# A recurrent attention layer and a mixture of experts in one kernel: the order of chunks 2 to 21, as written or from a list made at build time

## The chip, the cores and the metric

The kernel runs on one NeuronCore of a Trainium2 chip. The metric is the device time of one execution in microseconds (us); lower is better. A core has five engines, each of which takes its own instructions strictly in the order of the program: PE (matrix products, which write to the PSUM banks), DVE (vector work), ACT (scalar engine: copies and activations), POOL (vector work without access to PSUM, and DMA issues) and SP (DMA issues only). Engines wait for each other through semaphores that the Tile framework places from the data that instructions read and write.

## What is computed

The first half is a recurrence over 768 steps, for 4 batches and 8 heads, with a 40x40 state each; the second half sends every row of its result through a top-1 mixture of 8 experts:

```python
for t in range(768):
    y[:, :, t] = einsum('bhd,bhde->bhe', r_t, state)
    Sa = einsum('bhde,bhe->bhd', state, a_t)
    state = state * w_t[:, :, None, :] - einsum('bhd,bhe->bhde', Sa, b_t)
    state = state + einsum('bhd,bhe->bhde', v_t, k_t)
x = y as 3072 rows of 320
rows with x @ w_skip > 0: e = argmax(x @ w_gate), g = softmax weight of e
    out = x + g * (relu(x @ w1[e]) @ w2[e]);   other rows: out = x
```

## The kernel before, in words

The 768 steps are cut into 24 chunks of 32 steps. Inside a chunk the recurrence becomes matrix products, and only the state is handed from chunk to chunk. All heads are worked on at once, in two halves, x = 0 and x = 1 (of the head pairs), which are independent of each other.

For each chunk c and half x there is a chain. `rs` (L288) multiplies the state with the reads; its result goes from PSUM into the operand tile R1 (L292 on DVE when c is even, L293 on ACT when it is odd). `ux` (L302) multiplies R1, ACT copies the result (L304), `uq` (L313) applies the inverted triangular matrix, ACT writes it back into R1 in four copies (L315) and POOL masks it (L317). `sst` (L325, L330) makes the next state, which is copied out by L334 (DVE) or L335 (ACT), and by L338 (ACT); the next chunk's `rs` needs these. `yy` (L348) gives the output, which DVE scales (L352) and SP stores (L353).

Beside the chain runs preparation for later chunks, in pieces of two chunks (index h): DVE scans the decays (L114, L126), POOL multiplies keys and a (L143, L151), `m1` makes the triangular matrices on PE (L163), ACT and DVE empty its bank (L165, L174), POOL masks (L170) and SP moves the result by four DMAs of 32 KB (L172). `kbt` (L185, emptied by four ACT copies, L188), `wtt` (L197, emptied by L199) and `m2` (L207, emptied by four copies, L209) transpose and multiply other operands. For each piece of four chunks, `tinv` inverts the triangular matrices on DVE by 30 steps of forward substitution in two column blocks, X0 in PSUM (`px`) and Xi in SBUF (`M`): a product (L228) and a subtraction (L230) for each block and step. `route` scores finished rows for the experts (transposition L628, scores L636, selection L644 to L681 on DVE) and scatters them (L684).

The order of all this is written out by hand in the loop over c (L465): pieces of preparation stand between the links of the chain, the steps of `tinv` are given out by `T()`, those of `route` by `RP()`. PE, ACT and DVE issue in exactly the written order (a manual schedule); for POOL and SP the framework's own scheduler sets the order.

Eight PSUM banks are handed out by `Ring`, round robin, by purpose: two banks `pc` for rs, ux and uq; two `ps` for sst; one `py` for yy; one `px` for tinv; and two banks `pq` for everything else (m1, kbt, wtt, m2, route). A task that takes a bank waits until the one that had it before has been copied out.

Chunks 0 and 1 follow a start-up section of their own; chunks 22 and 23 run while the first expert's weights are split. Then come the experts (L744), whose matrix products fill PE.

## Time and profile before

| | us |
|---|---|
| median of three runs | 665.6 (663.45 to 666.89) |
| the profiled execution | 663.83 |
| its span, first to last instruction | 662.1 |
| busy in the span: PE / DVE / ACT / POOL | 515.5 / 489.7 / 419.5 / 324.2 |

The output rows of chunk c are scaled on DVE (L352) in the pass of the loop after it. The first of these 24 instructions starts at 92.5 us, the 21st at 481.8 and the last at 520.6, so one can cut the span by them: up to 92.9 us start-up and chunk 0; then twenty passes up to 482.3; then the end of the attention; and from about 530 the experts. In the listings a line such as `L228` is the line of the kernel printed above; `M<-M,px` reads "written tile from read tiles". PE's products of 16 small matrices appear as 32 records.

### The profile page before, as it was taken

What the parts mean: (1) busy time and instruction counts of PE and PEld (TensorE: products, weight loads), DVE (VectorE), ACT (ScalarE), POOL (GpSimd) and SP (SyncE); (2) the same over time, 40 slices, a digit from 0 to 9 for tenths busy, and PEclk for the clock granted to TensorE, in tenths of its full rate; (3) what the DMA queues carried; (4) which work ended last, traced back from release to release, by engine and by line L of the source; (5) the groups of instructions that cost most, each with busy time, mean ns of one, the idle gap of its engine ahead of it and who ended that gap; (6) DMA issues with size and microseconds to landing.
All of it is one profiled execution on the core that took longest, in us unless ns stands there. A gap on an engine that the chain in (4) does not pass through costs nothing.

```text
span 662.1 us, 33508 instructions
## 1 busy us (share of the span) xinstructions
PE 515.5 (78%) x14772; PEld 432.2 (65%) x14772; DVE 489.7 (74%) x1182; ACT 419.5 (63%) x1151; POOL 324.2 (49%) x246
## 2 busy tenths in 40 slices
PE   4777776676776787767785877878886899999995
PEld 1543456565664576656664666666775599999995
DVE  7998697858997479973999736864166457888881
ACT  5463674586965778567785677887885354555540
POOL 5481951648545375553946442223132155666661
PEclk8786895799977898878889689988788999999998
DMA  7473665352443525335253333453365266676210
GB/s 227 152 242 107 166 207 160 104 177 63 139 125 107 174 63 150 109 112 168 83 156 88 107 113 81 140 153 113 105 178 167 73 183 201 214 229 216 77 48 24
DMA packets 67446, 91.06 MB, mean 138 GB/s; under 512 B 32564, under 2 KB 54657, under 8 KB 65806
## 3 DMA queue, kind: packets, MB, share of 16 engines
q1 hardware_dynamic: 62350, 74.05, 38.1%
q0 software_dynamic: 4944, 14.80, 6.6%
q8 instruction: 118, 1.93, 1.2%
q14 instruction: 34, 0.28, 0.1%
HBM read 74.03 MB, written 17.08 MB: 138 GB/s over the span
## 4 chain that ended last, share of the span: by engine, by line
PE 24%; DVE 11%; ACT 8%; issue 5%; DMA 2%; POOL 1%; SPq 0%; POOLq 0%; DVEq 0%; ACTq 0%
PE pc L782 5%; PE ps L793 4%; PE px L782 3%; ACT R1t L315 2%; PE py L793 2%; ACT L2t L188 2%; DVE M L228 2%; PE ps L325 2%; DVE ti L789 2%; PE pc L313 1%; PE pc L288 1%; DVE M L230 1%; PE ps L330 1%; ACT SS L338 1%; ACT R1t L209 1%
## 5 line engine op out<-in xcount | busy, mean ns | idle before, releaser
L317 POOL TENSOR_TENSOR R1t<-R1t,mc 64x512 f32<-64x512 f32 x46 | 60.5, 1315 | 104.7 <-ACT R1t L315 72.6
L315 ACT COPY R1t<-pc 32x288 f32<-32x288 f32 x192 | 74.9, 390 | 20.7 <-PE pc L313 17.6
L730 POOL TENSOR_TENSOR WL<-WR,WH 128x1280 fp32r<-128x1280 f32 (+1 forms) x21 | 57.7, 2782 | 8.7 <-ACT WH L729 8.6
L188 ACT COPY L2t<-pq 64x160 f32<-64x160 f32 x184 | 52.8, 287 | 7.5 <-PE pq L185 5.1
L684 POOL DMA_INDIRECT xg<-XS,ix x24 | 25.5, 1064 | 64.3 <-DMA xg<-XS,ix 26.0
L325 PE MATMUL ps<-R1t,L2t 128*40 128x40 f32 x1472 | 48.2, 221 | 11.0 <-issue 5.3
L143 POOL TENSOR_TENSOR WR<-WR,M 128x1024 f32<-128x1024 f32 (+1 forms) x19 | 44.2, 2332 | 25.8 <-DVE M L114 19.7
L228 DVE TENSOR_TENSOR M<-M 128x22 f32<-128x22 f32 (+10 forms) x110 | 55.0, 500 | 0.0
L325 PEld LDWEIGHTS ps<-R1t,L2t 128*40 128x40 f32 x1472 | 39.3, 132 | 18.9 <-ACT R1t L315 8.9
L338 ACT COPY SS<-ps 40x320 f32<-40x320 f32 x92 | 38.7, 420 | 19.9 <-PE ps L330 18.5
L209 ACT COPY R1t<-pq 32x128 f32<-32x128 f32 x184 | 47.2, 256 | 5.5 <-PE pq L207 1.3
L288 PE MATMUL pc<-rvt,SS 128*40 128x32 f32 x1472 | 44.9, 216 | 7.2 <-issue 4.8
L288 PEld LDWEIGHTS pc<-rvt,SS 128*40 128x40 f32 x1472 | 38.3, 135 | 15.4 <-issue 7.8
L330 PE MATMUL ps<-L2t,R1t 128*40 128x40 f32 x1472 | 42.9, 218 | 6.5 <-issue 6.4
L313 PE MATMUL pc<-UXs,TB 32*32 32x72 f32 x1536 | 43.1, 255 | 6.0 <-issue 5.9
L330 PEld LDWEIGHTS ps<-L2t,R1t 128*40 128x40 f32 x1472 | 38.2, 134 | 7.3 <-issue 7.2
L230 DVE TENSOR_TENSOR M<-M 128x22 f32<-128x22 f32 (+10 forms) x110 | 40.8, 371 | 0.0
L230 DVE TENSOR_TENSOR px<-px,M 128x168 f32<-128x168 f32 (+8 forms) x150 | 39.1, 260 | 1.4
L729 ACT CAST WH<-WR 128x1024 fp32r<-128x1024 f32 (+1 forms) x35 | 39.6, 1132 | 0.0
L313 PEld LDWEIGHTS pc<-UXs,TB 32*32 32x32 f32 x1536 | 32.1, 122 | 11.4 <-issue 8.9
L789 DVE CAST ti<-xe 128x2 int32<-128x2 f32 x8 | 39.3, 4911 | 0.2
L174 DVE STREAM_TRANSPOSE M<-pq 128x128 f32<-128x128 f32 x40 | 12.1, 308 | 36.9 <-ACT M L165 24.3
(240 smaller groups left out, 1529.3 us busy)
## 6 DMA issues: line engine op xcount, KB each, us to landing
rvt<-rv POOLq DMA_DIRECT2D x21, 512.0 KB, 3.9
WR<-kb SPq DMA_DIRECT2D x10, 1024.0 KB
WR<-w SPq DMA_DIRECT2D x16, 640.0 KB
WR<-w SPq DMA_DIRECT2D x16, 512.0 KB
M<-wt SPq DMA_DIRECT2D x9, 520.5 KB
M<-at SPq DMA_DIRECT2D x8, 512.0 KB
WR<-w SPq DMA_DIRECT2D x16, 256.0 KB
R1t<-vt SPq DMA_DIRECT2D x48, 80.0 KB
```

Of the source, the lines that this page charges most:

```text
L188: A.copy(L2[x][h%NL2][64-64*x:128-64*x,c,bb*4:bb*4+4,:],pt[64*c:64*c+64,:,64*x:64*x+40])
L209: A.copy(R1[x][c%NR1][ao[x]:ao[x]+32,4*b:4*b+4,40:72],Pp[32*b:32*b+32])
L228: V.tensor_tensor(tv,NLt[:,j,j+1:32].unsqueeze(2).broadcast_to([128,n,k]),X[:,j,lo:hi].unsqueeze(1).broadcast_to([128,n,k]),ALU.mult)
L230: for tv,xv in q: V.tensor_tensor(xv,xv,tv,ALU.subtract)
L288: TE.matmul(RS[s,v,:],SS[x][:,b//2,v,:],rr[:,b%2,2*hh+x,:],start=True,stop=True)
L313: TE.matmul(UQ[q,hh,:],Tb[q,x*8+hh*2+c%2,:],UXd[x][q,hh,:],start=True,stop=True)
L315: A.copy(R[uu,4*b:4*b+4,:],UQ[32*b:32*b+32,:,:])
L317: (V if c==NC-1 else G).tensor_tensor(R[pq,:,40:72],R[pq,:,40:72],mQ[pq].unsqueeze(1).broadcast_to([64,16,32]),ALU.mult)
L325: TE.matmul(ST[s,v,:],l2[:,cc,u,:],R[:,u,0:40],start=True,stop=True)
L330: TE.matmul(S2[s,v,:],R[:,u,0:40],l2[:,cc,u,:],start=True,stop=True)
L730: def low(s,E,o,x,h): E.tensor_tensor(s.R(o),x,h,ALU.subtract)
L782: for n,(a,b) in enumerate(mm): TE.matmul(ph[:,g],R(a),R(b),start=n==0,stop=n==7)
```

## The change

Nothing that is computed changes. A recording layer is put between the loop and the engines (`Rec`). From c == 2 on, a call such as `V.tensor_tensor(...)` is no longer issued but written down as a task, with the parts of tiles that it reads and writes and a price from a table of formulas (`cost`); matmuls that follow each other into the same bank are one task. When c reaches 22, `flush` works out which task depends on which (`deps`), gives each a key (its place in the writing, times the busiest engine's work per task, less the priced length of the longest path from it to the end of the recording), and runs a list schedule (`plan`): each engine in turn takes the ready task with the lowest key, or one that fits in front of it with at most 1.0 us of delay. Then all tasks are issued in the order of their planned starts. POOL's order is now also fixed by this; SP's still comes from the framework's scheduler, which now sees the DMAs in the order of the plan.

Banks are handed out by the plan too. The rings for `pc`, `ps` and `pq` become three tiles of two banks each; a recorded task that wants a bank may get any of these six, with one pair held back for the oldest task that has none yet. `px` and `py` stay as they are. The pools of small tiles become fixed tiles used in turn (`Static`).

```diff
+class Rec:
+    HOP=0.12; PW=1.25
...
+    def cost(s,e,op,w,r,a):
...
+        if 'dma' in op:
+            by=4*n*min(128,w[0].ap[0][1])
+            return (0.06 if e=='S' else 1.0 if 'ind' in op else 0.6),2.0+by/2.6e5
+        if e=='P': return (0.145 if op=='transpose' else max(0.0005*sz(w[0]),0.058)),0
+        if e=='A': return 0.15+0.00085*n,0
+        if e=='G': return (0.08+n*0.0008 if op=='memset' else 0.65+0.0015*n),0
...
+        if op=='tensor_tensor': return 0.14+0.00105*n*(1 if ps else 1.6),0
...
+    def call(s,e,op,fn,a,k):
+        if not s.on: return fn(*a,**k)
...
+        if e=='P' and L and L.e=='P' and L.out==W[0][0]:
+            L.calls.append((fn,a,k,own)); L.W+=W; L.R+=R; L.d+=d; return
+        t=Task(); t.e,t.op,t.calls,t.W,t.R,t.d,t.lat,t.out=e,op,[(fn,a,k,own)],W,R,d,lat,W[0][0] if W else None
+        s.tasks.append(t)
...
+        while done<N:
+            best=None
+            for e in 'VAGPS':
+                c=[]
+                for i in pool[e] if not keep else [i for i in pool[e] if i==seq[e][nxt[e]]]:
+                    w=want(i) if T[i].al else (0.0,None)
+                    if w is None: continue
+                    c.append((max(free[e],rdy[i],w[0]),i,w[1]))
+                if not c: continue
+                c.sort(key=lambda x:s.key[x[1]])
+                x=c[0]
+                while True:
+                    f=[y for y in c if y[0]<x[0] and y[0]+T[y[1]].d<=x[0]+s.LET]
+                    if not f: break
+                    x=f[0]
+                if best is None or x[0]<best[0]: best=x+(e,)
...
+    LET=1.0; FAR=1.0
+    def keys(s):
+
+        w=max(sum(t.d for t in s.tasks if t.e==e) for e in 'VAGP')/len(s.tasks)
+        s.key=[i*w-s.FAR*t.up for i,t in enumerate(s.tasks)]
+    def flush(s):
+        s.on=False
+        s.deps(); s.keys(); s.plan()
...
+        for i in sorted(range(len(s.tasks)),key=lambda i:(s.st[i],i)):
+            for fn,a,k,own in s.tasks[i].calls: fn(*[at(x,own) for x in a],**{n:at(x,own) for n,x in k.items()})
...
-    ps_c,ps_s,ps_y,ps_p,ps_x=(Ring(pp,n,k) for n,k in (("pc",2),("ps",2),("py",1),("pq",2),("px",1))); m.ps=ps_p
+    PQ,PC,P2=(pp.tile([128,2,512],F32,name=n) for n in ("pq","pc","ps")); PY,PX=(pp.tile([128,512],F32,name=n) for n in ("py","px"))
+    rec.pairs={t.name:t for t in (PQ,PC,P2)}
+    two=lambda t: [t[:,q] for q in range(2)]
+    ps_c,ps_s,ps_p=(Ring(two(t),rec) for t in (PC,P2,PQ)); ps_y,ps_x=Ring([PY]),Ring([PX]); m.ps=ps_p
...
             ph,j=divmod(c,4)
+            if c==2: rec.on=True
             if c==20: m.load(0)
             if c==22:
+                with tc.manual_schedule(engines={ET.Pool}): rec.flush()
                 mp.__exit__(None,None,None)
```

Three places show what it does to the order. A row is one instruction, or several equal ones (`x16`); in the changed kernel every recorded instruction carries line 225, that of the issuing loop, or 115.

First PE, in a chunk in the middle, with four transpositions of `kbt` (shape 128x104). Before, each link of the chain has its fixed banks, and the rest shares `pq_104` and `pq_105`:

```order
L313 MATMUL pc_99<-UXs,TB 32x72 x16
L185 MATMUL pq_105<-mc,WR 128x104 x4
L348 MATMUL py_103<-L2t,R1t 32x40 x16
L636 MATMUL pq_104<-wg,xT 32x9 x12
L302 MATMUL pc_100<-R1t,WR 32x72 x16
L185 MATMUL pq_105<-mc,WR 128x104 x4
L325 MATMUL ps_102<-R1t,L2t 40x40 x16
L330 MATMUL ps_101<-L2t,R1t 40x40 x16
L207 MATMUL pq_104<-rvt 32x32 x16
```

and with the change, at the like place (`pq`, `pc` and `ps` name pairs of banks here):

```order
L225 MATMUL pq<-UX_447,TB 32x72 x16
L225 MATMUL ps<-WR,L1t 32x64 x16
L225 MATMUL pc<-mc,WR 128x104 x4
L225 MATMUL py<-L2t,R1t 32x40 x16
L225 MATMUL pq<-rvt_146 32x32 x16
L225 MATMUL pq<-mc,WR 128x104 x4
L225 MATMUL pc<-L2t,R1t 40x40 x16
L225 MATMUL pc<-R1t,L1t 32x72 x16
```

The transpositions and `m1` (32x64) now go into `pc`, `ps` and `pq` alike, and the two products of sst (40x40) no longer stand together.

Second DVE, in the midst of `tinv`. Before, the four instructions of a step alternate between the two blocks, so that an instruction never follows the one whose result it needs:

```order
L228 TENSOR_TENSOR M<-M,px_106 128x168
L228 TENSOR_TENSOR M<-M 128x130
L230 TENSOR_TENSOR px_106<-px_106,M 128x168
L230 TENSOR_TENSOR M<-M 128x13x10
L228 TENSOR_TENSOR M<-M,px_106 128x160
L228 TENSOR_TENSOR M<-M 128x132
L230 TENSOR_TENSOR px_106<-px_106,M 128x160
```

With the change:

```order
L225 TENSOR_TENSOR M<-M,px 128x168
L225 TENSOR_TENSOR px<-px,M 128x168
L225 TENSOR_TENSOR R1t<-ps,D_498 40x8x40 x2
L225 TENSOR_TENSOR M<-M 128x126
L225 TENSOR_TENSOR XS_1341<-py,WT_475 128x320
L225 TENSOR_TENSOR M<-M 128x14x9
L225 TENSOR_TENSOR M<-M,px 128x160
```

The product for `px` and its subtraction now stand next to each other, and the block in `M` runs several steps behind. Over the recorded chunks `tinv` has 508 such instructions in both orders; 70 of them follow directly the one whose result they need before, 154 now.

Third SP, in a stretch with one piece's slices (L172, from `at` into the tile that m1 reads next) and the loads of v (L107). Before:

```order
L172 DMA L1t<-M 32x256 x4
L107 DMA R1t<-vt 32x16x40
L94 DMA M<-wt 128x1041
L353 DMA out<-XS 4x32x320
L353 DMA X<-XS 4x32x320
L172 DMA L1t<-M 32x256 x4
L107 DMA R1t<-vt 32x16x40
```

With the change:

```order
L225 DMA R1t<-vt 32x16x40
L225 DMA WR<-M 32x256 x2
L225 DMA out<-XS_1342 4x32x320
L225 DMA X<-XS_1342 4x32x320
L225 DMA WR<-M 32x256 x4
L225 DMA M<-zer 32x1024
L225 DMA WR<-M 32x256 x2
L225 DMA R1t<-vt 32x16x40
```

The slices of the two halves x are mixed with stores and with each other; a load of v still stands behind slices.

## The prediction

> **What bounds the kernel now.** I read the page first, then busy time by stage, then four passes of the loop one by one, then what PE waited for.

> ```profile
> span 662.1 us, 33508 instructions
> PE 515.5 (78%) x14772; PEld 432.2 (65%) x14772; DVE 489.7 (74%) x1182; ACT 419.5 (63%) x1151; POOL 324.2 (49%) x246
> ```

> The busy times by stage (columns: stretch, its length, busy PE, weight loads, DVE, ACT, POOL, then granted PE clock, DMA share, GB/s):

> ```profile
> 0.00:92.90 92.90, 63.22 (x1686) 39.18 (x1688) 79.39 (x114) 51.32 (x138) 56.84 (x49) 0.83 0.59 181
> 92.90:482.30 389.40, 291.64 (x10956) 242.65 (x10951) 286.05 (x876) 281.44 (x853) 181.39 (x151) 0.87 0.42 122
> 482.30:530.00 47.70, 37.43 (x1207) 29.07 (x1207) 28.08 (x87) 26.42 (x81) 12.54 (x10) 0.89 0.49 144
> 530.00:662.10 132.10, 123.19 (x936) 121.31 (x936) 96.16 (x108) 60.33 (x81) 73.42 (x37) 0.98 0.48 149
> ```

> The change touches the second row alone. There no engine is full: PE 75%, DVE 73%, ACT 72%. The experts below are bound by PE (93%) and stay. So the question is what 389.4 us hold beside work. Four passes, one piece of `tinv`, show it, and with them the last pass of the stage:

> ```profile
> 218.10:244.10 26.00, 19.57 (x725) 16.40 (x725) 13.59 (x28) 17.73 (x53) 13.17 (x12) 0.87 0.43 123
> 244.10:259.30 15.20, 11.75 (x433) 9.75 (x425) 14.93 (x50) 13.18 (x41) 9.13 (x8) 0.89 0.48 139
> 259.30:286.50 27.20, 18.44 (x739) 15.35 (x733) 26.68 (x70) 17.35 (x53) 16.22 (x14) 0.86 0.43 126
> 286.50:300.20 13.70, 10.95 (x361) 8.92 (x361) 8.95 (x41) 9.80 (x32) 4.75 (x4) 0.78 0.33 91
> 466.00:482.30 16.30, 14.23 (x483) 12.09 (x478) 2.05 (x12) 14.56 (x44) 2.80 (x4) 0.79 0.36 107
> ```

> In the second and third pass DVE is full (41.6 of 42.4 us); in the first and fourth it is busy for 22.5 of 39.7 and nothing is full. The load is uneven, not too large: over the four passes PE has 60.7, DVE 64.2, ACT 58.1 us of work in 82.1. The last row shows that a pass can run with PE and ACT at 87% and 89%.

> What PE waited for in the stage (in total, times, longest):

> ```profile
> PE pq L628 <- DVE M L174: 12.3, 5, 4.1
> PE pq L163 <- issue: 11.1, 10, 3.3
> PE pc L302 <- DVE R1t L292: 11.0, 7, 2.9
> PE pq L207 <- ACT L2t L188: 9.7, 8, 1.4
> PE ps L325 <- issue: 5.3, 5, 2.1
> PE pq L185 <- ACT L2t L188: 5.2, 8, 1.6
> PE pq L636 <- ACT WT L199: 5.2, 5, 1.7
> PE py L348 <- issue: 5.0, 4, 2.0
> PE pc L288 <- issue: 4.8, 4, 1.6
> PE ps L325 <- ACT R1t L315: 4.0, 11, 0.5
> PE pc L302 <- issue: 3.9, 3, 1.8
> PE pc L313 <- issue: 3.6, 5, 1.4
> PE pq L671 <- ACT WT L199: 2.6, 9, 0.3
> PE pq L163 <- DVE M L174: 1.6, 1, 1.6
> ```

> Three kinds. Six rows say "issue": 33.7 us, PE waiting for nothing that the profile shows. Six name a bank `pq` that another task's copy has not emptied: 12.3 + 9.7 + 5.2 + 5.2 + 2.6 + 1.6 = 36.6. Two are links of the chain, 11.0 + 4.0 = 15.0. Smaller rows are left out; these 85 us stand against 97.8 idle (389.4 less 291.6).

> **The change part by part.** No instruction is added or removed, so PE's 291.6 us and the "issue" time stay: it touches only the 36.6 and 15.0 us, and may disturb what is hidden now.

> *Banks.* A task that found `pq` full now finds any of six banks, in a planned order. The rows that wait for ACT sum to 22.7; ACT has 108 us idle in the stage, so its copies can be in time, and I take 18 off (bounds 0 and 22.7). The rows that wait for DVE's L174 (13.9) are of another sort: that instruction stands behind `tinv` work while DVE is full, and a fuller PE does not change this. With six banks the PE task need not follow it, but the m1 behind it must; I take 6 off (bounds 0 and 13.9). Sum 24.

> *Chain.* The plan lets an evacuation with a long path behind it pass `tinv` steps. That can take at most the 15.0 us of L292 and L315. An evacuation still waits for the DVE instruction that is running, and the four L315 copies are work, not waiting. I take a third, 5 (bounds 0 and 15).

> *DVE neighbours.* The price table does not know that a DVE instruction directly behind the one whose result it needs starts later:

> ```profile
> 126.54 0.23 DVE L228 TENSOR_TENSOR M<-M,px 128x88 f32<-128x88 f32 x1
> 126.70 0.21 DVE L228 TENSOR_TENSOR M<-M 128x60 f32<-128x60 f32 x1
> 126.83 0.24 DVE L230 TENSOR_TENSOR px<-px,M 128x88 f32<-128x88 f32 x1
> 126.99 0.20 DVE L230 TENSOR_TENSOR M<-M 128x60 f32<-128x60 f32 x1
> 127.12 0.23 DVE L228 TENSOR_TENSOR M<-M,px 128x80 f32<-128x80 f32 x1
> ...
> 129.23 0.20 DVE L228 TENSOR_TENSOR M<-M,px 128x48 f32<-128x48 f32 x1
> 129.47 0.22 DVE L230 TENSOR_TENSOR px<-px,M 128x48 f32<-128x48 f32 x1
> 129.72 0.20 DVE L228 TENSOR_TENSOR M<-M,px 128x40 f32<-128x40 f32 x1
> ```

> Alternating, starts are 0.145 us apart (0.58 for four); in a single chain 0.245, though the tiles are smaller. So a neighbour costs 0.1 or a little more, say 0.11. The new order has 84 more of them (154 less 70): 9 us of DVE time. They are on the path only while DVE is full, which is half of the four passes (42.4 of 82.1): 4 us added (bounds 0 and 9). [...]

> *Clock.* After the longest of the L628 waits PE runs slowly for a while:

> ```profile
> 125.71 0.90 PE L628 MATMUL pq<-mc,XS 128*128 128x128 f32 x3 [4.14 <-DVE M L174]
> 126.54 1.28 PE L288 MATMUL pc<-rvt,SS 128*40 128x32 f32 x32
> ...
> 237.68 0.81 PE L288 MATMUL pc<-rvt,SS 128*40 128x32 f32 x32
> ...
> 125.70:129.00 3.30, 3.29 (x68) 2.65 (x69) 3.20 (x20) 1.26 (x4) 0.78 (x1) 0.50 0.49 147
> ```

> The granted clock was 0.50 there, and the same group took 1.28 us in place of 0.81. A stretch of 3.3 us so loses about 1.3 us; if all five of these waits went, 6 us; I take 3 (bounds 0 and 6). [...]

> *Loads.* SP's order changes too. PE's list has no row above 0.3 us that ends on a DMA, so I add nothing; what it would cost is a rival below.

> Sum against the profiled execution: 663.8 - 18 - 6 - 5 + 4 - 3 = 635.8. The median of the runs lies 1.8 us above that execution (665.6 against 663.83), so the forecast is 637.6, about 638. The stage would then last 361 us, in which PE's work and all its "issue" waits fill about nine tenths, against 84% now.

> **The rivals.**

> *The clock stays up.* If PE's idle pieces get so short that the half clock mostly disappears, more is won. A mean of 0.87 is a quarter of the stage, some 100 us, at half clock. If 60 us of these went, at three quarters busy and with 1.28 against 0.81 for the same work, 60 x 0.75 x 0.37 = 17 us would go beside the 28, less the 3 counted already: 624. For it: only the long waits have a slow stretch right behind them. Against: the last pass above has PE at 87% and a clock of 0.79.

> *DVE holds the pace.* `tinv` must be done before the next piece, and the DVE rows that lie between two scalings of output (L352) are almost as many as before in each pass. If the two full passes keep their length, only the other half gains: 24 + 5 by 39.7/82.1 is 14, less the whole 9 us of neighbours: 659 + 2 = 661, or with two thirds of that gain 665, that is, no change.

> *SP holds the chain.* The plan prices an issue on SP at 0.06 us. The trace:

> ```profile
> SPq L172 <- POOL M L170: 95.4, 15, 13.2
> ...
> 235.10 2.50 SPq L172 DMA_DIRECT2D L1t<-M  x4
> 237.69 0.59 SPq L107 DMA_DIRECT2D R1t<-vt  x1
> ```

> An issue takes about 0.6, and SP already stands for 6.4 us on average (95.4/15) before a group of slices, with the load of v for the next chunk behind it. Without v neither `ux` nor `sst` of that chunk can start, and all engines stop behind them. Today the load comes early enough. If the fuller order starts a chunk sooner but POOL's mask (L170) is no sooner, part of these waits lands on the chain. From 28/15 = 1.9 us each the change is slower; if half of each arrives, 15 x 3.2 = 48, it is 638 + 48 = 686. For it: stores now stand among the slices, ahead of the loads. Against: the loads have a whole pass of lead, and POOL is under half busy.

> **How the numbers follow.** Forecast (638, own range 622 to 653): 0.58. Clock stays up (624 and below): 0.15. No change (DVE): 0.11. Slower (SP, or another queue in the same way): 0.16. A measurement of this kernel tells a difference from about 0.5%, 3.3 us. Faster is then 0.73, same 0.11, slower 0.16. With every gain at its bound (22.7 + 13.9 + 15 + 6) the time is 606 + 2; I set the low end at 606. The high end is 668, which holds the no-change case and leaves most of the slower one out: about 0.05 and 0.14 outside.

> **What would show it.** Right: the passes of the recorded chunks last 17 to 19 us on average in place of 19.5; in PE's waits the rows that now end on L188, L199 and L174 shrink from 36.6 to about 12, and "issue" stays near 40; the experts keep their 132 us. For the clock: a granted clock above 0.92 in the stage. For DVE: two passes of four still as long as now, with DVE full. For SP: PE rows `pc` waiting for a DMA of v. I would be wrong altogether if waiting on "issue" grew with a denser PE, since nothing in the trace says what it is, or if new head-of-line waits between ACT and PE took the place of the bank waits.

## The result, and the profile after

The changed kernel takes 810.67 us (median; 806.66 to 816.17), the kernel before, run beside it, 664.72 us (663.45 to 666.89). The ratio is 1.22, with a 95% interval of 1.2105 to 1.229. The forecast was 638 us, faster. The profiled execution took 813.72 us. All times and ratios from here on are those of runs within 1.5% of the fastest of their kernel, since a few executions fall into a slower state.

The head of the page, and of its table of the span in 40 slices the rows for TensorE's work and granted clock:

```profile
span 812.0 us, 33448 instructions
PE 579.8 (71%) x14772; PEld 485.2 (60%) x14772; DVE 455.5 (56%) x1182; ACT 423.3 (52%) x1151; POOL 317.2 (39%) x246
...
PE   4687668676767667677768777776676777668776
...
PEclk8876767589767869876876869595687899889889
```

Busy times by stage, cut at the same instructions as before (start-up to the first scaling of output, the recorded chunks, the end of the attention, the experts):

```profile
0.00:105.70 105.70, 69.89 (x1672) 43.28 (x1673) 76.89 (x115) 52.89 (x138) 56.88 (x49) 0.75 0.53 162
105.70:550.80 445.10, 321.15 (x11005) 268.17 (x11002) 292.87 (x882) 283.24 (x851) 176.60 (x151) 0.77 0.36 108
550.80:609.50 58.70, 41.67 (x1172) 32.30 (x1168) 25.52 (x78) 25.99 (x81) 10.52 (x9) 0.73 0.36 107
609.50:812.00 202.50, 147.09 (x940) 141.41 (x940) 60.21 (x109) 61.17 (x83) 73.21 (x37) 0.88 0.32 98
```

Against the stages before, the start-up is 12.8 us longer, the recorded chunks 55.7, the end of the attention 11.0 and the experts 70.4. Most of the loss (94.2 of 149.9 us) therefore lies where nothing is recorded and every engine has the written order. In the experts, the last slices of the PE row show 6 to 8 tenths where there was a 9 throughout.

What TensorE waited for in the whole span (us in total, times, longest), largest rows:

```profile
PE pq L225 <- ACT R1t L225: 33.9, 36, 6.6
PE pc L115 <- DVE hL L115: 26.3, 12, 3.5
PE pq L115 <- DVE xH L115: 19.3, 7, 2.8
```

and all of its waits in the experts before:

```profile
PE pq L759 <- DMA xe<-xg: 1.0, 3, 0.6
PE px L782 <- DVE xL L730: 0.2, 1, 0.2
```

L225 issues what was recorded, L115 what was not. The second and third row are the experts': 45.6 us of waits for DVE instructions `hL` and `xH` that had no row before. The place where one of them falls, DVE's row first, then TensorE's:

```profile
617.13 0.68 DVE L115 SCALAR_TENSOR_TENSOR hL<-pc,hH 128x512 fp32r<-128x512 f32 x1
...
614.00 0.28 PE L115 MATMUL pc<-xH,WH 128*128 128x256 f32 x1
614.11 0.28 PE L115 MATMUL pc<-xH,WL 128*128 128x256 f32 x1
617.87 0.58 PE L115 MATMUL pc<-xH,WH 128*128 128x256 f32 x1 [3.48 <-DVE hL L115]
618.25 0.42 PE L115 MATMUL pc<-xH,WL 128*128 128x256 f32 x1
618.47 0.41 PE L115 MATMUL pc<-xH,WH 128*128 128x256 f32 x1
618.68 0.41 PE L115 MATMUL pc<-xH,WL 128*128 128x256 f32 x1
```

TensorE fills the first bank `pc` until 614.4. The products that follow go into the *second* bank `pc`, which is empty, and need nothing of `hL`; still they begin when DVE has finished reading the first bank, at 617.81. Before, the same two groups ran back to back, without a wait (the last product of the first and the first of the second):

```profile
533.71 0.28 PE L782 MATMUL pc<-xH,WL 128*128 128x256 f32 x1
533.82 0.28 PE L782 MATMUL pc<-xH,WH 128*128 128x256 f32 x1
```

In the change the rows behind the wait are 0.21 us apart instead of 0.12. The granted clock (the third number from the end) ahead of the wait's end and behind it, and of the same work before:

```profile
613.60:616.90 3.30, 0.79 (x7) 0.58 (x6) 2.74 (x3) 2.03 (x3) 0.00 (x0) 1.00 0.47 115
617.90:621.40 3.50, 3.50 (x16) 3.50 (x17) 0.00 (x0) 0.00 (x0) 0.00 (x0) 0.50 0.56 174
```

```profile
531.90:535.70 3.80, 3.80 (x34) 3.75 (x33) 1.94 (x3) 3.08 (x4) 0.00 (x0) 1.00 0.67 191
```

So the loss has two parts: the waits, and the half clock behind them. In the experts the work of PE grew by 23.9 us (147.09 against 123.19) for the same products, at a mean granted clock of 0.88 against 0.98, in the recorded chunks by 29.5 (321.15 against 291.64), at 0.77 against 0.87: a third of the whole loss. The wait lasted 3.48 us, but by the trace's clock records the clock fell at 617.0, 0.9 us before the wait ended, and TensorE had been busy for 0.79 of the 3.30 us ahead: that stretch was not wholly idle. The last section has more on this.

The instructions as built show why: each carries the semaphores it waits for. Before, none of TensorE's waits on ACT, DVE or POOL is owed to an instruction that only touches another bank. In the change 149 of some 520 are. It holds the other way too: 69 of ACT's 389 waits for TensorE and 18 of DVE's 115 end with products into the other bank; before, none did. The change cuts the six banks `pq`, `pc`, `ps` out of three tiles of two banks, and the framework that places the semaphores keeps the order of writes and reads by tile, so that a write into one half of a tile waits for the readers of the other half.

### The profile page after: what moved, and what is told of

The parts are those of the page before. It is cut to its first block, busy times and chain, and to the rows that moved or that the text cites. A ratio compares the mean times of both kernels' runs of the same rounds, so it can differ in the third digit from the quotient of the medians.

```text
span 812.0 us, 33448 instructions
## 1 busy us (share of the span) xinstructions
PE 579.8 (71%) x14772; PEld 485.2 (60%) x14772; DVE 455.5 (56%) x1182; ACT 423.3 (52%) x1151; POOL 317.2 (39%) x246
## 3 DMA queue, kind: packets, MB, share of 16 engines
q8 instruction: 118, 1.93, 1.0%
## 4 chain that ended last, share of the span: by engine, by line
PE 28%; ACT 12%; DVE 6%; issue 3%; DMA 1%; SPq 0%; POOL 0%; POOLq 0%; DVEq 0%; ACTq 0%
PE pc L115 7%; PE ps L115 6%; PE pq L225 6%; ACT R1t L225 4%; PE py L115 3%; PE pc L225 2%; ACT WH L115 2%; PE px L115 2%; ACT R1t L115 2%; DVE M L225 1%; PE pq L115 1%; DVE hL L115 1%; ACT L2t L225 1%; DVE WL L115 1%; PE ps L225 1%
## 5 line engine op out<-in xcount | busy, mean ns | idle before, releaser
L225 ACT COPY R1t<-pq 32x288 f32<-32x288 f32 (+3 forms) x260 | 87.2, 335 | 46.2 <-PE pq L225 35.0
L225 POOL TENSOR_TENSOR R1t<-R1t,mc 64x512 f32<-64x512 f32 x40 | 52.6, 1315 | 97.1 <-ACT R1t L225 74.9
L115 POOL TENSOR_TENSOR WL<-WR,WH 128x1280 fp32r<-128x1280 f32 (+1 forms) x21 | 57.5, 2738 | 79.8 <-ACT WH L115 52.7
L225 DVE TENSOR_TENSOR M<-M 128x130 f32<-128x130 f32 (+10 forms) x202 | 83.0, 411 | 1.9
L115 ACT ACTIVATE hH<-pc 128x512 fp32r<-128x512 f32 x21 | 12.5, 597 | 86.2 <-PE pc L115 86.2
L115 PE MATMUL pc<-xH,WH 128*128 128x256 f32 x126 | 35.8, 305 | 26.3 <-DVE hL L115 26.3
L225 ACT COPY R1t<-pc 32x128 f32<-32x128 f32 (+3 forms) x124 | 41.8, 337 | 21.8 <-PE pc L225 18.7
L115 PEld LDWEIGHTS pc<-xH,WH 128*128 128x128 f32 x126 | 25.2, 200 | 28.8 <-DVE hL L115 28.7
L225 POOL DMA_DIRECT2D rvt<-rv x20 | 11.9, 596 | 75.5 <-PE pc L225 42.6
L115 DVE TENSOR_TENSOR WL<-WR,WH 128x1024 fp32r<-128x1024 f32 (+1 forms) x19 | 23.8, 1253 | 28.9 <-ACT WH L115 25.8
L225 POOL TENSOR_TENSOR WR<-WR,M 128x1024 f32<-128x1024 f32 x14 | 32.0, 2291 | 20.5 <-DMA WR<-kb 17.1
L225 POOL DMA_INDIRECT xg<-XS,ix x20 | 24.4, 1219 | 39.8 <-DVE base L225 10.5
L115 ACT CAST WH<-WR 128x1024 fp32r<-128x1024 f32 (+1 forms) x35 | 39.4, 1125 | 0.0
L225 DVE TENSOR_TENSOR px<-px,M 128x168 f32<-128x168 f32 (+8 forms) x141 | 37.0, 263 | 2.6
L225 DVE TENSOR_TENSOR_SCAN M<-M 128x1041 f32<-128x1041 f32 (+1 forms) x14 | 37.1, 2653 | 0.4
L225 DVE TENSOR_TENSOR M<-M,px 128x168 f32<-128x168 f32 (+8 forms) x141 | 35.0, 248 | 1.6
L225 PE MATMUL pq<-UX,TB 32*32 32x72 f32 x928 | 27.0, 266 | 9.8 <-issue 2.8
L115 POOL DMA_INDIRECT out<-ro,ti x16 | 15.7, 982 | 44.2 <-DVE ro L115 30.9
L115 PE MATMUL ps<-WH,hH 128*128 128x320 f32 x88 | 31.0, 352 | 1.9 <-DVE ro L115 1.9
L225 DVE TENSOR_TENSOR R1t<-pc,D 40x256 f32<-40x256 f32 (+1 forms) x38 | 16.7, 439 | 25.9 <-PE pc L225 17.8
L115 DVE SCALAR_TENSOR_TENSOR hL<-pc,hH 128x512 fp32r<-128x512 f32 x21 | 14.5, 688 | 29.5 <-ACT hH L115 29.5
L225 PE MATMUL pc<-rvt,SS 128*40 128x32 f32 x800 | 25.9, 228 | 7.0 <-ACT L2t L225 2.8
```

What stands on the lines that cost most here:

```text
L115: if not s.on: return fn(*a,**k)
L225: for fn,a,k,own in s.tasks[i].calls: fn(*[at(x,own) for x in a],**{n:at(x,own) for n,x in k.items()})
```

## The experiments

Theory A: the false waits between the two banks of a tile make the loss, whatever the order. Rivals: the list's order makes it (B), or the fixed tiles that replace the pools' rings (C).

**e1_single: the list schedule on six tiles of one bank.** The order of TensorE, DVE and ACT is the change's, instruction for instruction.

```diff
-    PQ,PC,P2=(pp.tile([128,2,512],F32,name=n) for n in ("pq","pc","ps")); PY,PX=(pp.tile([128,512],F32,name=n) for n in ("py","px"))
+    bk=lambda n,k: [pp.tile([128,512],F32,name=f"{n}{q}")[:,0:512] for q in range(k)]
+    PQ,PC,P2=(bk(n,2) for n in ("pq","pc","ps")); PY,PX=(bk(n,1)[0] for n in ("py","px"))
...
```

> The list schedule of the change with its order untouched; only the three pairs of banks are six tiles of one bank each again. Theory A (two banks in one tile make TensorE wait for readers of the other bank): the 52 us of the start-up, the end and the experts come back, the experts take about 132 us instead of 203, TensorE's waits named pq and pc fall under 40 us in the recorded stage, and the time is 620 to 668 us, 638 as first forecast. Theory B (the list's order is what costs): the recorded stage stays near 445 us, and the time is 740 to 815 us. Theory C (the fixed tiles in place of the pools' rings cost): start-up and experts stay slow, about 750 us or more.

668.85 us, ratio 1.0104 (1.0065 to 1.0144). The recorded chunks and the experts:

```profile
92.40:483.10 390.70, 292.42 (x10975) 246.10 (x10972) 303.52 (x882) 282.14 (x848) 174.21 (x151) 0.86 0.41 122
...
531.50:662.20 130.70, 122.70 (x939) 121.53 (x938) 92.71 (x110) 60.31 (x81) 73.43 (x37) 0.99 0.49 151
```

All of the large loss is gone, in the experts too. (The three stages outside the recorded chunks had grown by 94 us, not by the 52 that the expectation names.) But the time is a little above theory A's range, and the waits for the banks `pq` and `pc` in the recorded chunks still come to 57.8 us without issue, not to under 40: the list's order itself gains nothing, the recorded chunks last 390.7 us against 389.4. That is a second question, taken up below.

**e2_pairs_only: the kernel before, with three tiles of two banks.**

```diff
-    ps_c,ps_s,ps_y,ps_p,ps_x=(Ring(pp,n,k) for n,k in (("pc",2),("ps",2),("py",1),("pq",2),("px",1))); m.ps=ps_p
+    PQ,PC,P2=(pp.tile([128,2,512],F32,name=n) for n in ("pq","pc","ps"))
+    ps_c,ps_s,ps_p=(Ring.of([t[:,q] for q in range(2)]) for t in (PC,P2,PQ)); ps_y,ps_x=(Ring(pp,n,1) for n in ("py","px")); m.ps=ps_p
```

> The kernel before in its written order; only its six rotating banks are cut out of three tiles of two banks, as in the change. Theory A: slower everywhere, the experts 190 us or more instead of 132 and the whole 740 to 860 us, since the rings give the two banks of a tile out in turn. Theory B and theory C: 662 to 668 us, no difference from before.

909.34 us, ratio 1.3702 (1.3642 to 1.3762), above the range: the written order uses the two banks of a tile in turn everywhere, so it suffers more (262 of TensorE's waits are owed to the other bank). The experts take 203.8 us, and their two rows are those of the change, almost to the tenth:

```profile
PE pc L783 <- DVE hL L786: 26.4, 12, 3.5
...
PE pq L760 <- DVE xH L763: 19.3, 7, 2.8
```

**e3_single_norec: fixed tiles, six banks apart, nothing recorded.** The line `if c==2: rec.on=True` and the call of `flush` are left out of e1_single.

> The changed kernel with the recording never switched on (so every engine has the written order) and with six tiles of one bank: what is left of the change is the fixed tiles in place of the pools' rings. Theory A and theory B: 662 to 668 us. Theory C: more than 675 us.

662.94 us, ratio 0.9995 (0.9965 to 1.0025): theory C falls. With e1 and e2, theory A is shown: the tiles alone slow the written order, and with them apart the order costs about 1% and the fixed tiles nothing that can be measured.

Then why does the order gain nothing, where 28 us were forecast? In the rows of TensorE in the recorded chunks I count a wait as one for a bank if the tile waited for is not among the row's operands, and as one for data if it is. "Neighbours" are DVE tensor-tensor instructions directly behind the one whose result they need. All in us but the last two columns:

| kernel | stage | bank | data | issue | DVE busy | neighbours | ratio to before |
|---|---|---|---|---|---|---|---|
| before | 389.4 | 37.6 | 17.1 | 39.9 | 286 | 103 | 1 |
| the change | 445.1 | 94.5 | 13.5 | 14.5 | 293 | 189 | 1.2197 (1.2105 to 1.229) |
| e3_single_norec | 385.7 | 38.7 | 21.9 | 28.2 | 286 | 103 | 0.9995 (0.9965 to 1.0025) |
| e4_banks_only | 380.3 | 11.3 | 31.4 | 45.8 | 282 | 103 | 0.9888 (0.985 to 0.9926) |
| e5_order_only | 404.0 | 61.1 | 9.7 | 27.1 | 304 | 198 | 1.0185 (1.0134 to 1.0236) |
| e1_single | 390.7 | 52.3 | 9.9 | 34.1 | 304 | 189 | 1.0104 (1.0065 to 1.0144) |
| e9_neighbours_only | 384.0 | 60.6 | 9.7 | 28.3 | 276 | 49 | 0.9976 (0.9943 to 1.0008) |
| e7_prices_no_neighbours | 384.0 | 41.7 | 9.7 | 43.2 | 301 | 201 | 0.9789 (0.9744 to 0.9835) |
| e6_prices | 374.9 | 36.3 | 8.9 | 33.6 | 290 | 31 | 0.9729 (0.9696 to 0.9762) |
| e8_port | 368.5 | 12.1 | 9.0 | 60.7 | 270 | 112 | 0.9718 (0.9661 to 0.9775) |
| e12_port_flat | 369.2 | 32.2 | 7.3 | 42.9 | 266 | 152 | 0.9727 (0.9671 to 0.9784) |

Each row is one profiled execution. e3_single_norec has the order and the banks of before, so its row shows how far two executions can lie apart: 4 us in the stage, 5 in the waits for data, 12 in issue.

**e4_banks_only: the term Banks by itself.** TensorE, DVE and ACT keep the written order; only the bank of each recorded task is chosen anew, the one that has been free for longest.

```diff
...
+        for o in sorted(us,key=lambda o:us[o][0]):
+            k=min(fr,key=lambda k:(fr[k],k)); assert fr[k]<us[o][0]; s.bank[o]=k; fr[k]=us[o][1]
...
-        for i in sorted(range(len(s.tasks)),key=lambda i:(s.st[i],i)):
+        for i in range(len(s.tasks)):
```

> Written order on TensorE, DVE and ACT, six tiles of one bank, but each task of chunks 2 to 21 gets the bank of the six that has been free for longest. This is the forecast's term Banks alone. Theory B1 (a full bank pq is what TensorE waits for): 18 to 24 us less than the kernel before, 640 to 647 us, and the waits for a bank (37 us in the stage) fall to about 12. Theory B2 (the copy that empties the bank is late, so TensorE waits for the next thing that the same copy holds up): 657 to 666 us, and the waits for a bank turn into waits for data.

659.03 us, 1.1% faster. The waits for a bank fall from 37.6 to 11.3 us, as B1 said, but the time is B2's: the stage gains only 9.1, and waits for data take back 14.3 and issue 5.9 (the last within the spread of two executions). TensorE's rows in the stage name the next obstacle, the evacuations of the chain and, first of all, issue:

```profile
PE pc L224 <- issue: 17.6, 17, 3.6
PE ps L224 <- issue: 12.9, 16, 2.1
PE pq L224 <- issue: 10.6, 12, 1.8
PE ps L224 <- DVE R1t L224: 9.8, 5, 2.9
```

**e5_order_only: the list schedule, each task kept to its own two banks.** In e1_single, in the planner's rule for a free bank:

```diff
-            ok=lambda k,o: k[0]!=res or o==old[0] or s.first[o]==res
+            ok=lambda k,o: k[0]==s.first[o]
```

> The list schedule on six tiles of one bank, made with the rule that a task may only have one of the two banks that it had in the written order. Theory B1: the order without the freedom of banks is worth little or nothing, 663 to 675 us, and slower than the list schedule with six banks (668.85). Theory B2 (banks are not what limits): the same as the list schedule with six banks, 664 to 672 us.

680.29 us, 1.85% slower: a little above B1's range, and against B2. The two effects add, within their intervals: 0.9888 x 1.0185 is 1.007, and both together (e1) are 1.0104. The order costs about 12 us, and the freedom of banks gives 5 to 7.5 back; the list is made anew under each rule for banks, so e5's order is not quite e1's.

**e6_prices, e7_prices_no_neighbours, e9_neighbours_only: the planner's table.** Six banks apart and free, the table of prices corrected from the traces:

```diff
-        if e=='P': return (0.145 if op=='transpose' else max(0.0005*sz(w[0]),0.058)),0
+        if e=='P':
+            y=tuple(tuple(d) for d in w[0].ap)
+            if op=='transpose': return (0.17 if y[-1][1]==104 else 0.25),0
+            return {(40,40):.062,(40,32):.058,(32,72):.052,(32,40):.0355,(32,32):.033,(32,9):.045}.get((y[0][1],y[-1][1]) if len(y)==2 else 0,.05),0
...
-            t.up=t.d*s.PW+max([s.tasks[j].up+t.lat+(s.HOP if s.tasks[j].e!=t.e else 0) for j in t.n],default=0)
-    def edge(s,a,b): return a.lat+(s.HOP if a.e!=b.e or a.lat else 0)
+            t.up=t.d*s.PW+max([s.tasks[j].up+s.edge(t,s.tasks[j]) for j in t.n],default=0)
+    def edge(s,a,b): return a.lat+(s.HOP if a.e!=b.e or a.lat else 0)+(0.17 if a.e=='P' and b.e!='P' else 0.09 if a.e=='V' else 0)
```

SP's issue goes from 0.06 to 0.6, the HOP from 0.12 to 0.1. The path lengths in the keys (`up`) now count these edges too. e7 has 0 for the 0.09; e9 has the change's table with the 0.09 alone, in the plan and in the keys.

> The list schedule with six free banks of one tile each; only the table of prices is changed to what the traces show: products of TensorE by their shape (0.033 to 0.062 us instead of 0.058 for all, transposes 0.17 and 0.25 instead of 0.145), 0.17 us from the end of a TensorE group to its reader, 0.09 us between a DVE instruction and the next one that needs its result, 0.6 us for an issue on SP instead of 0.06. Theory C1 (the schedule gained nothing because its table is wrong, TensorE 10% too dear and neighbours on DVE free): the recorded stage falls from 391 us to 355 to 370, and the time is 632 to 648 us. Theory C2 (any fixed order loses what it gains, because instructions vary in length when DVE and POOL or the clock interfere): 660 to 672 us.

> As e6_prices, but a DVE instruction may again stand directly behind the one whose result it needs at no price: 201 such pairs in chunks 2 to 21 instead of 31. With the forecast's price of 0.11 us each, 170 more pairs are 19 us of DVE time. [...]

> The change's own table of prices on six tiles of one bank, with one thing added: 0.09 us between a DVE instruction and the next one that needs its result (49 dependent neighbours in chunks 2 to 21). Theory N1 (the neighbours are what the list order lost on): 8 to 12 us less than the list schedule's 668.85, 655 to 661 us. Theory N2 (the price of TensorE's products is what it lost on): 664 to 670 us.

e6_prices takes 648.32 us, 2.7% faster than before: the order was bad because its table was. It is just above C1's times, its stage (374.9) is above C1's 355 to 370, and C2's 660 to 672 is out; whether C2's reason holds for the rest is not shown. e7_prices_no_neighbours takes 653.9 us, 5.6 more than e6, where the expectation has 19 us more of DVE time. The two ratios' intervals overlap, so a cost of the neighbours is likely here, but not shown. DVE is busy 10.7 us longer with 170 more of them, 0.063 us each instead of the forecast's 0.11. The two plans differ elsewhere too, so 0.063 is an estimate, and other things move DVE's time as much: e8_port has 81 neighbours more than e6 and 20.9 us less. e9_neighbours_only takes 661.94 us, ratio 0.9976, between N1 and N2: against e1_single 6.9 us come back. What the remaining step to e6 owes to which price was not taken apart.

**e8_port: the plan also keeps POOL's work and DVE's work on two operands in SBUF apart.** In e6_prices, first DVE, then POOL:

```profile
251.22 0.26 DVE L222 TENSOR_TENSOR M<-M 128x112 f32<-128x112 f32 x1
251.40 0.34 DVE L222 TENSOR_TENSOR px<-px,M 128x184 f32<-128x184 f32 x1
251.66 1.11 DVE L222 TENSOR_TENSOR M<-M 128x112 f32<-128x112 f32 x1
...
254.16 0.33 DVE L222 TENSOR_TENSOR px<-px,M 128x168 f32<-128x168 f32 x1
254.40 2.03 DVE L222 TENSOR_TENSOR M<-M 128x126 f32<-128x126 f32 x1
...
251.36 1.28 POOL L222 TENSOR_TENSOR R1t<-R1t,mc 64x512 f32<-64x512 f32 x1 [2.75 <-ACT R1t L222]
254.06 2.22 POOL L222 TENSOR_TENSOR WR<-M 64x1024 f32<-64x1024 f32 x1 [1.42 <-PE pc L222]
```

The `M<-M` rows have both operands in SBUF. The first starts before POOL and takes 0.26; the other two start while POOL works and last until 0.13 and 0.15 us after POOL's instruction has ended (252.64 and 256.28); the `px` rows beside them, with an operand in PSUM, run through at 0.34 and 0.33. At 251.66 POOL had 0.98 us left and DVE's row took 1.11. (The expectation's 0.98 and 0.96 us are not the numbers of this row.) From the planner's new lines (`lk` marks DVE's two-operand instructions on SBUF and POOL's products and copies):

```diff
+                    if T[i].lk:
+                        h=hold['G' if e=='V' else 'V']
+                        if h[0]<=t0<h[1]: t0=h[1]
...
```

> As e6_prices, and the plan also knows that a DVE instruction that reads two tiles of SBUF and a POOL instruction on SBUF cannot run at the same time (in e6_prices such a DVE instruction took 0.98 us where POOL had 0.96 left to run, 0.24 otherwise). Theory D1 (what is left between plan and chip is this blocking): the recorded stage falls from 375 us to 345 to 362, the time to 620 to 637 us. Theory D2 (the blocking is hidden behind other waits): 643 to 652 us, as e6_prices.

644.61 us, ratio 0.9718: no different from e6_prices (0.9729), so D2. But the table shows that its reason is not the one expected. DVE's busy time falls by 21 us and the waits for a bank from 36.3 to 12.1; what stands in their place is issue, 60.7 us:

```profile
93.30:461.80 368.50, 284.87 (x10980) 239.99 (x10974) 269.52 (x881) 279.42 (x846) 176.98 (x150) 0.89 0.43 129
```

```profile
PE pq L230 <- issue: 24.5, 22, 3.3
PE pc L230 <- issue: 20.4, 17, 2.6
PE py L230 <- issue: 9.8, 7, 2.7
PE pq L230 <- ACT R1t L230: 6.8, 11, 1.3
PE ps L230 <- issue: 5.9, 4, 3.1
```

Busy and issue together are 345.6 of 368.5 us, 94%: TensorE is nearly full, in a way that its busy share (77%) does not show.

**e11_tail: what issue is.** In the recorded chunks of e8_port, matmul records counted from one issue wait to the next come to 128, or a whole multiple of it, within four, 47 times of 49 (before: 32 of 36; in e6_prices only 23 of 37). 128 records are 256 instructions with their weight loads. The page says of the queue that it calls `instruction` (packets, MB, share), for the kernel before and then for e11_tail:

```profile
q8 instruction: 118, 1.93, 1.2%
...
q8 instruction: 141, 2.31, 1.3%
```

1.93 MB in 118 packets are 16.4 KB each, and TensorE's 2 x 14772 instructions make 115 blocks of 256. To see the rate by itself, e11_tail has 2 x 768 small products behind the experts, 3072 records or 24 blocks, and 23 packets more:

```diff
...
+                grp(768,lambda u: T[u%3])
+                for q in range(24): nc.sync.dma_start(T[q%3],i['rv'][q].rearrange("p a b c -> p (a b c)") if len(i['rv'].shape)==5 else i['rv'][q])
+                grp(768,lambda u: m.idn)
```

> The kernel before with two groups of 768 products of 128x40 appended behind the experts (1536 matmul records each, results unused): the first with nothing else running, the second while SP loads 24 blocks of 512 KB. TensorE's waits on issue lay whole multiples of 128 records apart in the traces so far. Theory F1 (they are refills of TensorE's instruction store in blocks of 256 instructions, at a rate of their own): once the store has run dry, the first group shows a wait every 128 records, and takes 3.5 to 4 us for each 128 instead of 128 x 0.018 = 2.3. Theory F2 (the refill shares the DMA engines with the loads): the second group takes 5 us or more for each 128. Theory F3 (issue is something of the kernel's own waits): no such pattern here, both groups run at 2.3 us for 128.

```profile
679.74 1.95 PE L895 MATMUL pc<-T 128*32 128x40 f32 x128 [2.11 <-issue]
683.50 2.36 PE L895 MATMUL pc<-T 128*32 128x40 f32 x128 [1.81 <-issue]
686.98 2.36 PE L895 MATMUL pc<-T 128*32 128x40 f32 x128 [1.13 <-issue]
...
705.18 1.36 PE L895 MATMUL pc<-T 128*32 128x40 f32 x128 [1.39 <-issue]
708.93 2.36 PE L895 MATMUL pc<-T 128*32 128x40 f32 x128 [2.39 <-issue]
...
723.48 2.35 PE L895 MATMUL pc<-mc 128*32 128x40 f32 x128 [5.22 <-issue]
729.14 2.36 PE L895 MATMUL pc<-mc 128*32 128x40 f32 x128 [3.31 <-issue]
...
757.64 2.36 PE L895 MATMUL pc<-mc 128*32 128x40 f32 x128 [2.76 <-issue]
```

Two stretches, the first with nothing else running and the second under loads; the third and second number from the end are the granted clock and the DMA share:

```profile
696.00:700.00 4.00, 2.61 (x160) 2.45 (x153) 0.00 (x0) 0.00 (x0) 0.00 (x0) 0.50 0.02 4
720.00:740.00 20.00, 9.34 (x512) 8.79 (x512) 0.00 (x0) 0.00 (x0) 0.00 (x0) 0.50 0.85 281
```

A wait every 128 records, though nothing else runs in the first group. From 679.74 to 708.93 eight blocks take 29.2 us, 3.65 each, at a DMA share of 0.02; from 723.48 to 757.64 seven take 34.2, 4.9 each, at 0.85. The wait is not a matter of how long the products take: at 705.18 a block ran in 1.36 us instead of 2.36, and the next still came 3.75 us after it. So the waits and the times that F1 names are there (in one run), and F2 is right in its direction, a little under its 5 us. That the waits are fetches of instructions is inferred from the numbers of the queue, 16.4 KB a packet and 23 packets more for 24 blocks; no record shows what ends one. A packet itself takes 1.1 us (1.3% of 16 engines' 775.2 us, over 141 packets); what fills the rest of the 3.65 stays open. The other traces fit: in the recorded chunks of ten kernels (before, e1, e3 to e9 and e12) no eight blocks in a row took less than 3.60 us each, and no 32 less than 4.08.

**e12_port_flat: e8_port with the change's flat price for TensorE.**

> As e8_port, but with the change's one price of 0.058 us for each product of TensorE (transposes 0.145); neighbours, POOL's blocking, 0.17 us to the reader and SP's 0.6 us stay mended. 0.058 us for a product is 3.7 us for 128 records, the rate at which issue waits followed each other. Theory G1 (the flat price stands for the refills, and is the better one): 5 us or more below e8_port, 630 to 640 us. Theory G2 (a price that is too dear for the short products puts other work behind them): 650 to 662 us.

650.6 us beside 670.88 of the kernel before in that comparison, ratio 0.9727: the same as e8_port and e6_prices. The time lies at the edge of G2's range, but the kernel before ran 7 us slower there than beside e8_port; by the ratio it is neither G1 nor G2, and the price of the products does not decide once the rest is mended.

**e10_prices_pairs: e6_prices with the change's tiles of two banks.**

> The mended prices of e6_prices, but with the change's three tiles of two banks. Theory A (the two faults add): 146 us more than e6_prices as the changed kernel stood 142 above the same order on single banks, so 780 to 805 us. If a better order could hide the false waits: under 760 us.

789.4 us, as theory A expected. The false waits (147 of TensorE's waits) cost as much on the good order (141 us above e6_prices) as on the change's (142 above e1_single): one fault does not hide the other.

e6_prices, e8_port and e12_port_flat are faster than the kernel before by the same 2.7 to 2.8%, and than the changed kernel by 160 us or more. That three plans end at the same gain would fit a common bound in the rate at which TensorE's blocks of 128 records follow each other; this is not shown.

## Why the prediction was wrong

- **"No instruction is added or removed … it touches only the 36.6 and 15.0", and "the experts … stay".** This step failed, and it is nearly the whole error. The list of instructions stayed, but what each waits for did not: with three tiles in place of six, 149 of TensorE's waits are owed to another bank, in all four stages (27, 79, 11 and 32). Measured: 142 us, as the difference between the change and e1_single, of which 48 in the experts are the waits themselves (1.2 us of waits before) and 24 half clock. I read in which order instructions stand, and not the semaphores they carry. None of the rivals had it either: the sentence on "new head-of-line waits between ACT and PE" came nearest, but it laid them to the order.
- **Banks, -24.** The mechanism is right and the size is wrong. By itself (e4_banks_only) the freedom of banks cuts these waits to 11.3 us, the 12 that I forecast, but is worth 7.5 us. I summed waits as if each were time of its own. Behind a free bank TensorE found the chain's evacuations and issue (waits for data of 31.4 us instead of 17.1, issue 45.8 instead of 39.9).
- **In the list order the bank waits grew** (52.3 us). Probably the copy that empties a bank stands in ACT's or DVE's list behind work that was planned too short, and more banks do not hurry it. That is argued and not shown by a run of its own; with the mended table the same waits are 36.3 us, and with POOL's blocking planned for 12.1.
- **Chain, -5.** Right: waits for data fall from 17.1 to 9.9 in e1_single, without effect on the sum.
- **DVE neighbours, +4.** Right in sign, a little small. DVE's busy time in the recorded chunks grew by 17.5 us instead of 9 (303.52 against 286.05), by neighbours and by POOL's blocking, which I had not seen; no run shows how it divides. Pricing the neighbours alone brought 6.9 us (e9 against e1); without that price e7 takes 5.6 more than e6, with intervals that overlap.
- **Clock, -3.** Wrong in its reading: half clock was laid to the long waits ("only the long waits have a slow stretch right behind them"). In the recorded chunks TensorE has 2 waits over 3 us before and 3 in the change, but the clock fell 20 times and 27 times. What grew is the number of waits, from 105 to 145 (94.7 to 122.5 us); the mean clock fell from 0.87 to 0.77, and with it went about 53 us (29.5 + 23.9) of the loss, here and in the experts.
- **"There no engine is full."** True of the busy shares, and not the whole of it. The 10,956 records of the recorded chunks are 85.6 blocks of 128. At 3.65 us each that is 312 us, 80% of the 389.4, an estimate of what no order goes below at that rate; at the DMA share of e8_port's chunks (0.43) a straight line between the two rates gives 4.27 us a block and 365 us (an estimate too), and its stage took 368.5. The 33.7 us of issue that I left as unexplained would belong to such a bound. I had written that I would be wrong if issue grew with a denser TensorE; it did in e8_port, from 39.9 to 60.7.
- **SP holds the chain.** Not seen: in e1_single the only row of TensorE that ends on a load of v has 1.7 us, once and ahead of the recorded chunks; the changed kernel has none. That the result was slower after all, to which this rival gave most of its 0.16, is no credit to it.

Which of the corrected prices beside the neighbours (TensorE's products and transpositions, 0.17 us to the reader, SP's 0.6, the path lengths) makes e6_prices faster stays open.

## What to carry to other kernels

When a change re-cuts buffers, count the semaphore waits of the built program by what they protect, before thinking about order: a tile that holds two independent buffers makes each wait for the other, also far from the code that was changed. Do not add up the waits of an engine as gains: free one kind alone, and see what it finds next. A list schedule is as good as its table; check the sums of its prices against the busy times of a trace, with what a per-instruction price leaves out: here the neighbours, and DVE's instructions that last as long as POOL's.
